# Two weight conversions moved between the stages of an attention and two-MoE kernel

## The chip, the cores and the metric

The kernel runs on one core of a Trainium2 chip. The metric is the device time of one execution in microseconds (us). Five engines of a core work side by side, each through its own instructions in their order: TensorE (PE), VectorE (DVE), ScalarE (ACT), GpSimd (POOL) and SyncE (SP), which issues all the DMA transfers here. They wait for one another by semaphores. An instruction whose input or whose buffer isn't ready holds up everything behind it on its engine.

## The reference

An attention over packed keys, then two layers called MoE, which are plain two-layer networks:

```python
p_packed = sm_attn(p, k, v)              # 8 batches, 8 heads, 576 positions, 64 wide
x = sm_attn(q, p_packed, p_packed)       # reshaped to 4608 x 512
h = x @ w_in1;  g = max(0.01*h, h);                y   = g @ w_out1   # 512 -> 2048 -> 512
h = y @ w_in2;  g = h / (1 + exp(-1.702*h));       out = g @ w_out2   # 512 -> 2048 -> 512
```

The weights come as 64-bit floats. The kernel turns them to 32 bits itself.

## The kernel before

**Stages.** (1) Attention and the first MoE's first layer, up to about 368 us; g goes to DRAM. (2) "y", the first MoE's second layer, 368 to 732 us. (3) "units", the second MoE's first layer, 732 to 1133 us. (4) "sum", its second layer, to the end.

**Seven products.** y, units and sum multiply 2 x 2 blocks by seven products instead of eight (`PRODUCTS`, in the order 1, 7, 5, 6, 2, 4, 3), with sums of the left and of the right quarters as operands. For each weight matrix, the seven combinations of its quarters are formed beforehand and put into a scratch in DRAM. Every operand is split into a high and a low part (fp32r): ScalarE casts the high part, DVE subtracts it from the value (L107). Each product is three matmuls: high x high, high x low, low x high.

**Steps.** The stages count in steps. In y a step is one slice of 128 of one product, 6 matmuls (line 650); a block of 768 tokens is 7 x 8 = 56 steps, and there are 6 blocks, so 336 steps. In the units a step is one product of one unit, also 6 matmuls (line 684); 48 units of 7 steps make 336 steps too. What is not matmul work stands in an agenda: `at(step, ...)` puts a piece at a step, and `side(step)` runs what is due there, in the order in which it was put there. So the order of each engine's instructions is a matter of these step numbers. `split(step, ...)` puts a cast on ScalarE at a step and the subtraction on DVE (L107) at the next.

**y.** For step k the left operand is cast at step k-3 and subtracted at k-2. DVE also forms the sums of quarters, each 768 wide: S3 at steps 1, 4, 7, 10 of a block (L480), S1 at 12, 14, 16, 19 (L482), S2 at 20, 22, 24, 27 (L484) and S4 at 34, 38, 42, 46 (L486), and adds results out of PSUM at the ends of products (L515 at step 23, L520 at 31, L525 at 47 and 55; L521 at 34 is without PSUM). In the last block, from step 28 on, `y_block` prepares the first block of y for the units as well, one piece every second step, and `new_weights` the first weights.

**Units.** Four pairs of PSUM banks. Products 1 and 2 of a unit share a bank, 7 and 4 another. ScalarE copies u out of the first after product 1 (L688) and v out of the second after product 7 (L690); the products 2 and 4, three steps later, go into the same banks behind these copies. `new_weights` converts the weights of the next unit pair in four pieces; `load_weights` fetches them from the scratch of w_in2. `y_block` prepares the next block of y in 14 pieces: slowly, every four steps (from steps 36 and 148), or fast, every one and a half (from steps 105 and 217). Each unit's g goes to DRAM two steps behind its end. From step 231 on, `weights` fetches and casts the first weights of sum ("early").

**A conversion.** `combined(what, first, late)` puts one `combine` of a 128-wide part at each step s of the list `first`: 16 for w_in2 (names wi), 16 for w_out2 (wo). Each has these pieces:
- s: three DMAs load the raw words (tile raw, one buffer; 512 KB in all).
- s+late: ScalarE's two casts L121 (into tile b) and L122 (into tile v).
- +1: DVE L125. +2: DVE L128, POOL's addition L129 into b.
- +5: DVE L144, L145. +6: DVE L147, L148.
- +7: the DMA that stores seven parts of b to the scratch (448 KB, L151).

Raw, v and b have one buffer each: the next conversion's loads wait for L128 of this one, and its L121 waits for this one's store to have landed.

Of the kernel before, what the change touches and what calls it, by code (L numbers as in the profile page):

```python
# [24 lines left out]
NJ = NF // 2  # L25
# [21 lines left out]
def packed_attention_moe_moe_kernel(tc, qT, kT, vm, vt, pT, w_in1, w_out1, w_in2, w_out2, out):  # L47
# [32 lines left out]
    with ExitStack() as ctx:  # L80
# [28 lines left out]
        def pieces(piece, steps):  # L109

            for step in steps:
                at(step, lambda: next(piece, None))
# [19 lines left out]
        def combine(name, source, scratch):  # L132


            conv = pools["conv"]
            raw = conv.tile([P, 4, 256], U32, tag="raw", name=f"raw_{name}")
            for i, (x, y) in enumerate(((0, 1), (0, 0))):
                nc.sync.dma_start(raw[:, i], source[:, x, y])
            nc.sync.dma_start(raw[:, 2:4], source[:, 1])
            yield  # L140
            b = conv.tile([P, 8, P], F32, tag="b", name=f"b_{name}")
            v = conv.tile([P, 4 * P], F32, tag="v", name=f"v_{name}")
            yield from to_f32(b[:, 0:4].rearrange("p i w -> p (i w)"), raw.rearrange("p i (w t) -> p (i w) t", t=2), v, True)
            nc.vector.tensor_sub(b[:, 4], b[:, 0], b[:, 1])  # L144
            nc.vector.tensor_sub(b[:, 5], b[:, 3], b[:, 0])  # L145
            yield
            nc.vector.tensor_sub(b[:, 6], b[:, 3], b[:, 4])  # L147
            nc.vector.tensor_sub(b[:, 7], b[:, 2], b[:, 6])  # L148
            if scratch is not wo1c:
                yield  # L150
                nc.sync.dma_start(place(name, scratch), b[:, 1:8])  # L151
                return
            yield
            h = pools["px"].tile([P, 2, 7, P], F32R, tag="hl", name=f"hl_{name}")
            nc.scalar.copy(h[:, 0], b[:, 1:8])
            yield
            nc.vector.tensor_sub(h[:, 1], b[:, 1:8], h[:, 0].bitcast(F32))
            yield
            for x in range(2):
                nc.sync.dma_start(place(name, scratch)[:, x], h[:, x].bitcast(F32))  # L160
# [2 lines left out]
            _, j, u = name.split("_")  # L163
            return scratch[int(j)][..., P * int(u):P * int(u) + P]

        def combined(what, first, late, start=0):

            view, to = {"wo1": (w_out1_v, wo1c), "wi2": (w_in2_v, wi2c), "wo2": (w_out2_v, wo2c)}[what]
            for n, s in enumerate(first, start):
                j, u = divmod(n, 2)  # L170
                src = view[:, :, u, :, j, :] if what == "wi2" else view[:, :, j, :, u, :]
                pieces(combine(f"{what}_{j}_{u}", src, to), (s, *(s + late + k for k in (0, 1, 2, 5, 6, 7, 8, 9))))
# [234 lines left out]
        for c in range(1, 4):  # L407
            for k in range(4):
                s = 8 * c - 8 + k
# [4 lines left out]
        for b in range(B):  # L414
            s = 32 * b
            if b + 1 < B:
                if b == 0:
                    first, second = (8, 9, 9, 10, 11, 12), range(14, 22)
                    third, fourth = range(22, 30), range(24, 32)
                else:  # L420
                    first, second = (-3, -2, -2, 0, 1, 2), range(5, 13)
# [7 lines left out]


        combined("wo1", range(30, 30 + 16 * 11, 11), 8)

        steps = [(blk, p, f) for blk in range(NBK) for p in PRODUCTS for f in range(NJ)]
# [40 lines left out]
        def prepare(nm, g):  # L474


            def combo(blk, fp, what):
                a11, a12, a21, a22 = (raws.get((blk, i, h, fp)) for i in range(2) for h in range(2))
                if what == "S3":
                    nc.vector.tensor_sub(a11, a11, a21)  # L480
                elif what == "S1":
                    nc.vector.tensor_add(a21, a21, a22)  # L482
                elif what == "S2":
                    nc.vector.tensor_sub(a11, a22, a11)  # L484
                else:
                    nc.vector.tensor_sub(a12, a12, a11)  # L486
                    load_raw(blk + 1, 0, 0, fp, nm, g)

            def high(k, blk, p, f):
                src = raws[(blk, *PLACE[p], f // 2)][:, f % 2, :]  # L490
                t = ga[blk, p, f] = pools["dr"].tile([P, 2, HB], F32R, tag=f"s{k % ROLL}", name=f"{nm}a_{blk}_{p}_{f}")
                nc.scalar.copy(t[:, 0, :], src)  # L492
                return t[:, 1, :], src, t[:, 0, :].bitcast(F32)

            for blk in range(NBK):
                s = 7 * NJ * blk
                for what, when in (("S3", (1, 4, 7, 10)), ("S1", (12, 14, 16, 19)), ("S2", (20, 22, 24, 27)), ("S4", (34, 38, 42, 46))):
                    for fp, k in enumerate(when):
                        at(s + k, lambda blk=blk, fp=fp, what=what: combo(blk, fp, what))
            for k, step in enumerate(steps):  # L500
                split(k - LEAD - 1, lambda k=k, step=step: high(k, *step))
                blk, p, f = step
                if f % 2 and p in (5, 4, 3):
                    at(k - LEAD, lambda blk=blk, p=p, f=f: load_raw(blk + 1, *PLACE[p], f // 2, nm, g))
# [34 lines left out]
        for k in range(EARLY):  # L539
            s = 32 * (B - 2) + 20 + 8 * k  # L540
# [29 lines left out]
        def y_block(early, steps, blk):  # L570

            t0 = TB * blk
            q = {}

            def load():
                for i, j in ((0, 0), (1, 0), (1, 1), (0, 1)):
                    home, tag = ("dr", f"r10{2 * i + j}") if blk == 0 else ("cy", f"y{2 * i + j}")
                    q[i, j] = pools[home].tile([P, 2, HB], F32, tag=tag, name=f"yq_{blk}_{i}{j}")
                    nc.sync.dma_start(q[i, j], yT[2 * j:2 * j + 2, :, t0 + HB * i:t0 + HB * i + HB].rearrange("d p t -> p d t"))

            def one(p, k):
                src, i = q[PLACE[p]], PRODUCTS.index(p)
                if blk not in ya:
                    ya[blk] = pools["ABC"[blk % 3]].tile([P, 7, 2, 2, HB], F32R, tag="ABC"[blk % 3], name=f"ya_{blk}")
                t = ya[blk][:, i]
                nc.scalar.copy(t[:, 0, k], src[:, k])
                return t[:, 1, k], src[:, k], t[:, 0, k].bitcast(F32)

            def combo(p):
                sub = nc.vector.tensor_sub  # L590
                if p == 1:
                    sub(q[0, 0], q[0, 0], q[1, 0])
                    nc.vector.tensor_add(q[1, 0], q[1, 0], q[1, 1])
                elif p == 7:
                    sub(q[0, 0], q[1, 1], q[0, 0])
                elif p == 6:
                    sub(q[0, 1], q[0, 1], q[0, 0])
            at(early, load)
            for n, step in enumerate(steps):
                p, k = (1, 2, 7, 5, 6, 4, 3)[n // 2], n % 2  # L600
                split(step, lambda p=p, k=k: one(p, k))
                if k:
                    at(step + 1, lambda p=p: combo(p))
# [29 lines left out]
        first_raws("b", g1)  # L633
        later_weights(lambda n: "w5" if n < 8 else "d", wo1c, "wo1")
        prepare("b", g1)
        combined("wi2", [56 * blk + k for blk in range(1, 5) for k in (-4, 14, 32)], 14)
        last = 7 * NJ * (NBK - 1)
        y_block(last + 24, range(last + 28, last + 56, 2), 0)
        side_until(0)
        for k, (blk, p, f) in enumerate(steps):  # L640
# [7 lines left out]
            for c in range(2):  # L648
                for m, (ws, xs) in enumerate(((0, 0), (0, 1), (1, 0))):
                    nc.tensor.matmul(acc[BANK[p]][:, c, :HB], lhsT=w[:, ws, P * c:P * c + P], rhs=x[:, xs, :],  # L650
                                     start=(p in OPENS and f + m == 0), stop=(f == NJ - 1 and m == 2), skip_group_check=True)
# [68 lines left out]
        for m in range(2, 3 * NJ - 1):  # L720
            late = (8 if (m + 1) % NJ == 2 else 4 if m == 2 else 0 if (m + 1) % NJ == 1 else 1)
            new_weights(range(14 * m + late, 14 * m + late + 4), m + 1)
        for q in range(2):
            s = 14 * NJ * q
            y_block(s + 28, range(s + 36, s + 92, 4), 2 * q + 2)
            y_block(s + 92, [s + 105 + 3 * n // 2 for n in range(14)], 2 * q + 3)
        combined("wi2", range(1, 49, 12), 11, 12)
        combined("wo2", range(49, 49 + 16 * 11, 11), 10)
        for k in range(EARLY):
            s = 7 * (4 * NJ + 2 * k + 1)  # L730
            weights(s, (s + 8, s + 12), k // 2, k % 2, None, wo2c, "wo2")
        at(7 * (6 * NJ - 3), *(lambda fp=fp: load_raw(0, 1, 0, fp, "d", g2) for fp in range(4)))
        at(7 * (6 * NJ - 1), *(lambda fp=fp: load_raw(0, 0, 0, fp, "d", g2) for fp in range(4)))
# [23 lines left out]
        for k, (blk, p, f) in enumerate(steps):  # L757
            side(k)
            x, w = ga.pop((blk, p, f)), wt[p, f // 4][:, :, f % 4]
            for c in range(3):  # L760
                b = acc4[BANK[p]][:, c // 2, 256 * (c % 2):256 * (c % 2) + 256]
                for m, (xs, ws) in enumerate(((0, 0), (0, 1), (1, 0))):
                    nc.tensor.matmul(b, lhsT=x[:, xs, P * c:P * c + P], rhs=w[:, ws, :],  # L763
                                     start=(p in OPENS and f == 0 and m == 0 and c != 1),
# [48 lines left out]
```

## Time and profile before

| what | value |
|---|---|
| median of 3 runs | 1504.54 us (1504.23 to 1504.83) |
| the profiled execution | 1506.49 us, its span 1504.7 us |
| PE busy | 1425.3 us, 95% of the span |
| DVE busy | 1102.7 us, 73% |
| ACT busy | 836.3 us, 56% |
| POOL busy | 95.8 us, 6% |
| L684, matmuls of the units | 2016, busy 369.9 us, idle before them 31.0 us |
| L650, matmuls of y | 1296 and 720, busy 231.0 and 128.9 us, idle before them 3.5 and 5.5 us |
| L763, matmuls of sum | 1944 and 1080, busy 233.2 and 132.4 us, idle before them 1.5 and 1.7 us |

Busy times say how long an engine had an instruction at work. Idle time before a group of instructions is the time for which their engine stood still ahead of them, and the releaser behind it is the instruction whose end let them start. Matmuls overlap, so a stretch is best judged by its length over its number of matmuls. PEld is the load of weights into the array, which precedes each matmul.

### The profile page before, as it was taken

Reading aid. Unit: us, or ns where it says so; the run is one execution under the profiler, and the core shown is the slowest. Engines: PE = TensorE matmul, PEld = TensorE weight load, DVE = VectorE, ACT = ScalarE, POOL = GpSimd, SP = SyncE. Lnnn points to the kernel's source line nnn. Section 1 sums busy time; section 2 is a strip of 40 time slices with the busy share of each in tenths; the row PEclk is TensorE's granted clock in tenths of the full one; section 3 lists DMA queues with packets and bytes.
Section 4 is the critical chain, followed back from the end, with each engine's and each line's share of the span. In section 5 each row is a group of like instructions: output and inputs, shape, how many; then the busy total and the mean of one; then the engine's idle time right before and its main releaser. Section 6 shows DMA issues by size and latency. Waiting matters only on the chain. (4 is left out here: it accounts for less than half of the span.)

```text
span 1504.7 us, 27724 instructions
## 1 busy us (share of the span) xinstructions
PE 1425.3 (95%) x10400; PEld 1329.5 (88%) x10400; DVE 1102.7 (73%) x2068; ACT 836.3 (56%) x1791; POOL 95.8 (6%) x71
## 2 busy tenths in 40 slices
PE   7789999999999999999999998889999999999998
PEld 4567777778999999999889988789999999999998
DVE  5667767762778888888877786676658987777876
ACT  3656666665555555455665665456655645445443
POOL 1310110000000101100011110100000000000000
PEclk7889999999999999999999999999999999999999
DMA  9459999969977366562466867585667524525321
GB/s 362 156 201 316 312 320 302 341 220 335 325 255 222 122 207 191 166 207 80 155 238 223 289 213 262 185 264 184 219 225 265 187 66 156 178 65 168 119 93 43
DMA packets 228773, 317.42 MB, mean 211 GB/s; under 512 B 12576, under 2 KB 188704, under 8 KB 228640
## 3 DMA queue, kind: packets, MB, share of 16 engines
q1 hardware_dynamic: 228640, 315.67, 63.0%
q8 instruction: 81, 1.33, 0.3%
q14 instruction: 52, 0.43, 0.1%
HBM read 191.89 MB, written 123.73 MB: 210 GB/s over the span
## 5 line engine op out<-in xcount | busy, mean ns | idle before, releaser
L684 PE MATMUL h<-ya,wj 128*128 128x384 f32 x2016 | 369.9, 344 | 31.0 <-ACT uv L688 13.7
L684 PEld LDWEIGHTS h<-ya,wj 128*128 128x128 f32 x2016 | 359.2, 192 | 41.5 <-ACT uv L688 17.7
L338 PEld LDWEIGHTS h<-a,m 128*128 128x128 f32 x1536 | 215.9, 195 | 53.5 <-ACT g L343 22.1
L338 PE MATMUL h<-a,m 128*128 128x288 f32 x1536 | 239.8, 309 | 9.3 <-ACT a L315 3.4
L492 ACT CAST da<-dr 128x384 fp32r<-128x384 f32 x336 | 166.4, 514 | 145.9 <-PE sum L763 108.1
L492 ACT CAST ba<-br 128x384 fp32r<-128x384 f32 x336 | 164.8, 514 | 142.7 <-PE y L650 83.4
L763 PE MATMUL sum<-wo,da 128*128 128x256 f32 x1944 | 233.2, 281 | 1.5 <-DVE da L107 1.3
L650 PE MATMUL y<-ba,wo 128*128 128x384 f32 x1296 | 231.0, 337 | 3.5 <-DVE ba L107 2.8
L763 PEld LDWEIGHTS sum<-wo,da 128*128 128x128 f32 x1944 | 231.0, 188 | 3.1 <-DVE da L107 3.1
L650 PEld LDWEIGHTS y<-ba,wo 128*128 128x128 f32 x1296 | 224.1, 188 | 9.5 <-DVE ba L107 8.4
L107 DVE TENSOR_TENSOR da<-dr,da 128x384 fp32r<-128x384 f32 x336 | 172.5, 552 | 40.9 <-ACT da L492 40.8
L107 DVE TENSOR_TENSOR ba<-br,ba 128x384 fp32r<-128x384 f32 x336 | 177.0, 565 | 32.3 <-ACT ba L492 32.2
L343 ACT ACTIVATE g<-h 128x288 f32<-128x288 f32 x256 | 105.4, 417 | 99.8 <-PE h L338 98.6
L650 PE MATMUL y<-ba,wo_early 128*128 128x384 f32 x720 | 128.9, 340 | 5.5 <-DVE ba L107 2.9
L763 PE MATMUL sum<-wo_early,da 128*128 128x256 f32 x1080 | 132.4, 285 | 1.7 <-ACT da L492 1.6
L763 PEld LDWEIGHTS sum<-wo_early,da 128*128 128x128 f32 x1080 | 131.5, 193 | 2.2 <-ACT da L492 1.9
L650 PEld LDWEIGHTS y<-ba,wo_early 128*128 128x128 f32 x720 | 126.3, 190 | 7.2 <-DVE ba L107 4.5
L327 DVE TENSOR_TENSOR m<-m,m 128x512 fp32r<-128x512 f32 x64 | 42.9, 683 | 54.8 <-ACT m L325 54.4
L129 POOL TENSOR_TENSOR b_wo<-v_wo,b_wo 128x512 int32<-128x512 int32 x32 | 43.1, 1348 | 418.6 <-DVE v_wo L128 248.7
L677 ACT ACTIVATE g<-cc 128x384 f32<-128x384 f32 x96 | 50.4, 525 | 29.1 <-DVE cc L700 26.2
L107 DVE TENSOR_TENSOR wj<-wjs,wj 128x512 fp32r<-128x512 f32 x88 | 54.5, 632 | 11.9 <-ACT wj L626 11.7
L129 POOL TENSOR_TENSOR b_wi<-v_wi,b_wi 128x512 int32<-128x512 int32 x16 | 30.4, 1898 | 447.6 <-DVE v_wi L128 347.6
(114 smaller groups left out, 1357.1 us busy)
## 6 DMA issues: line engine op xcount, KB each, us to landing
g_scratch<-g SPq DMA_DIRECT2D x64, 576.0 KB, 5.2
br<-g_scratch SPq DMA_DIRECT2D x96, 384.0 KB, 5.5
g_scratch<-g SPq DMA_DIRECT2D x96, 384.0 KB, 4.6
dr<-g_scratch SPq DMA_DIRECT2D x96, 384.0 KB, 4.4
wjs<-wi_scratch SPq DMA_DIRECT2D x22, 896.0 KB, 5.3
wo_scratch<-hl_wo SPq DMA_DIRECT2D x32, 448.0 KB, 5.9
wo<-wo_scratch SPq DMA_DIRECT2D x27, 512.0 KB, 8.7
k<-in_kT_dram SPq DMA_DIRECT2D x16, 576.0 KB, 6.6
```

Of the source, the lines that this page charges most:

```text
L107: at(step + 1, lambda: nc.vector.tensor_sub(*rest))
L129: nc.gpsimd.tensor_tensor(d, v.bitcast(I32), d, op=ALU.add)
L327: nc.vector.tensor_sub(m[:, 1, par, :], t[par], m[:, 0, par, :].bitcast(F32))
L338: nc.tensor.matmul(t[:, :TH], lhsT=m[:, ws, par, o:o + P], rhs=a[:, xs, par, :], start=(k == 0), stop=(k == 5))
L343: nc.scalar.activation(g1t[g][:, f % 2, hf * TH:hf * TH + TH], t[:, :TH], AF.Prelu, alpha=0.01)
L492: nc.scalar.copy(t[:, 0, :], src)
L650: nc.tensor.matmul(acc[BANK[p]][:, c, :HB], lhsT=w[:, ws, P * c:P * c + P], rhs=x[:, xs, :], start=(p in OPENS and f + m == 0), stop=(f == ...
L677: nc.scalar.activation(g[f][:, HB * i:HB * i + HB], src, AF.Gelu_apprx_sigmoid)
L684: nc.tensor.matmul(b, lhsT=w[:, ws, c, P * kk:P * kk + P], rhs=x[:, xs, kk, :], start=(p in OPENS and kk + s == 0), stop=(kk + s == 3), sk ...
L763: nc.tensor.matmul(b, lhsT=x[:, xs, P * c:P * c + P], rhs=w[:, ws, :], start=(p in OPENS and f == 0 and m == 0 and c != 1), stop=(f == NJ ...
```

## The change

Three lists of steps change, and a parameter that is no longer needed goes.

```diff
-        def combined(what, first, late, start=0):
+        def combined(what, first, late):
...
-        combined("wi2", [56 * blk + k for blk in range(1, 5) for k in (-4, 14, 32)], 14)
+        combined("wi2", [26, 44] + [56 * blk + k for blk in range(1, 5) for k in (1, 19, 38)] + [281, 299], 14)
...
-        combined("wi2", range(1, 49, 12), 11, 12)
-        combined("wo2", range(49, 49 + 16 * 11, 11), 10)
+        combined("wo2", range(3, 3 + 16 * 15, 15), 10)
         for k in range(EARLY):
-            s = 7 * (4 * NJ + 2 * k + 1)
+            s = 7 * (4 * NJ + 2 * k + 2)
```

- w_in2's 16 conversions all stand in y now: two that load in block 0 (steps 26 and 44), three in each of blocks 1 to 4 (at their steps 1, 19, 38 instead of -4, 14, 32), two in the last block (its steps 1 and 19). Before, the last four stood in the units, at steps 1, 13, 25, 37.
- w_out2's 16 conversions start at step 3 of the units instead of 49 and come every 15 steps instead of 11. The last loads at 228 instead of 214.
- The early weights of sum are fetched and cast one unit (7 steps) later.

The number of instructions of each kind stays the same.

ScalarE in the units, around units 20 and 21, before. b_wo and v_wo are the targets of a conversion's casts L121 and L122, uv those of the copies L688 and L690, g the results, ya the prepared y.

```order
L677 ACTIVATE g_20_1_9923<-uv_9920 128x384
L677 ACTIVATE g_20_0_9922<-cc_9921 128x384
L688 COPY uv_10003<-h_8312 128x384
L121 ACTIVATE b_wo_4_0_10014<-raw_wo_4_0_9895 128x512
L122 ACTIVATE v_wo_4_0_10015<-raw_wo_4_0_9895 128x512
L677 ACTIVATE g_20_1_9923<-cc_9921 128x384
L690 COPY uv_10003<-h_8313 128x384
L586 CAST ya_10026<-yq_00_9931 128x384
```

The same place now:

```order
L677 ACTIVATE g_20_1_9943<-uv_9940 128x384
L677 ACTIVATE g_20_0_9942<-cc_9941 128x384
L688 COPY uv_10019<-h_8376 128x384
L677 ACTIVATE g_20_1_9943<-cc_9941 128x384
L690 COPY uv_10019<-h_8377 128x384
L586 CAST ya_10038<-yq_00_9951 128x384
L121 ACTIVATE b_wo_4_1_10040<-raw_wo_4_1_9926 128x512
L122 ACTIVATE v_wo_4_1_10041<-raw_wo_4_1_9926 128x512
```

The conversion that stood between the two copies of one unit stands behind both now. With 15 steps between conversions and units of 7 steps, their place in a unit moves on by one step each time, so that others stand between the copies.

SP's queue in the units, where raw_wo is a load of raw words, b_wo the store of a finished conversion, wjs the next weights and g_scratch the stores of g, before:

```order
L614 DMA wjs_10151<-wi_scratch 128x1792
L138 DMA raw_wo_5_0_10154<-in_w_out_dram 128x256 x2
L139 DMA raw_wo_5_0_10154<-in_w_out_dram 128x2x256
L710 DMA g_scratch<-g_22_0_10086 128x768
L710 DMA g_scratch<-g_22_1_10087 128x768
L151 DMA wo_scratch<-b_wo_4_1_10138 896x1x128
L138 DMA raw_wo_5_1_10274<-in_w_out_dram 128x256 x2
L139 DMA raw_wo_5_1_10274<-in_w_out_dram 128x2x256
```

And now:

```order
L138 DMA raw_wo_5_0_10093<-in_w_out_dram 128x256 x2
L139 DMA raw_wo_5_0_10093<-in_w_out_dram 128x2x256
L151 DMA wo_scratch<-b_wo_4_1_10040 896x1x128
L710 DMA g_scratch<-g_21_0_10021 128x768
L710 DMA g_scratch<-g_21_1_10022 128x768
L614 DMA wjs_10163<-wi_scratch 128x1792
L710 DMA g_scratch<-g_22_0_10100 128x768
L710 DMA g_scratch<-g_22_1_10101 128x768
L138 DMA raw_wo_5_1_10257<-in_w_out_dram 128x256 x2
L139 DMA raw_wo_5_1_10257<-in_w_out_dram 128x2x256
```

The next loads of raw words stand farther behind the store.

DVE in the last block of y, steps 15 to 21 (br are the quarters with their sums, ba the subtracted left operands), before:

```order
L482 TENSOR_TENSOR br_102_7299<-br_102_7299,br_112_7559 128x768
L107 TENSOR_TENSOR ba_5_2_7852<-br_101_7277,ba_5_2_7852 128x384
L107 TENSOR_TENSOR ba_5_3_7864<-br_101_7277,ba_5_3_7864 128x384
L107 TENSOR_TENSOR ba_5_4_7873<-br_102_7299,ba_5_4_7873 128x384
L482 TENSOR_TENSOR br_103_7320<-br_103_7320,br_113_7579 128x768
L107 TENSOR_TENSOR ba_5_5_7882<-br_102_7299,ba_5_5_7882 128x384
L484 TENSOR_TENSOR br_000_7457<-br_110_7513,br_000_7457 128x768
```

And now:

```order
L107 TENSOR_TENSOR ba_5_2_7888<-br_101_7299,ba_5_2_7888 128x384
L125 TENSOR_SCALAR raw_wi_7_0_7750<-raw_wi_7_0_7750 128x512
L107 TENSOR_TENSOR ba_5_3_7904<-br_101_7299,ba_5_3_7904 128x384
L128 SCALAR_TENSOR_TENSOR v_wi_7_0_7891<-v_wi_7_0_7891,raw_wi_7_0_7750 128x512
L107 TENSOR_TENSOR ba_5_4_7914<-br_102_7299,ba_5_4_7914 128x384
L482 TENSOR_TENSOR br_103_7349<-br_103_7349,br_113_7611 128x768
L107 TENSOR_TENSOR ba_5_5_7925<-br_102_7299,ba_5_5_7925 128x384
L484 TENSOR_TENSOR br_000_7480<-br_110_7542,br_000_7480 128x768
L107 TENSOR_TENSOR ba_5_6_7935<-br_103_7349,ba_5_6_7935 128x384
L144 TENSOR_TENSOR b_wi_7_0_7890<-b_wi_7_0_7890 128x128
L145 TENSOR_TENSOR b_wi_7_0_7890<-b_wi_7_0_7890 128x128
```

A conversion's DVE instructions stand where there was none. In blocks 1 to 4 a conversion stood some five steps earlier and now stands at this place.

## Rows read from the trace of the kernel before

**Rows 1.** Stretches: us, busy of PE, PEld, DVE, ACT, POOL; clock; DMA share; GB/s.
```profile
367.80:428.60 60.80, 60.49 (x336) 59.92 (x337) 45.71 (x78) 30.99 (x62) 0.00 (x0) 0.97 1.02 344
...
732.20:758.40 26.20, 23.33 (x122) 20.63 (x121) 21.29 (x38) 17.30 (x37) 1.47 (x1) 1.00 0.62 214
758.40:1056.80 298.40, 270.24 (x1457) 262.44 (x1457) 213.28 (x439) 172.41 (x378) 25.69 (x19) 0.96 0.69 233
1056.80:1133.10 76.30, 76.29 (x438) 75.98 (x438) 41.41 (x77) 41.22 (x87) 0.00 (x0) 1.00 0.67 224
```
**Rows 2.** Groups by line, 758.4 to 1056.8: busy, mean ns | idle before, releasers.
```profile
L684 PE MATMUL h<-ya,wj 128*128 128x384 f32 x1457 | 270.2, 346 | 28.6 <-ACT uv L688 13.4 <-ACT uv L690 11.7 <-DVE uv L692 2.3
```
**Rows 3.** Timeline of PE in the units: start, us, what [idle before, releaser].
```profile
861.32 7.73 PE L684 MATMUL h<-ya,wj 128*128 128x384 f32 x42 [1.38 <-ACT uv L688]
...
881.96 28.00 PE L684 MATMUL h<-ya,wj 128*128 128x384 f32 x156 [0.81 <-DVE uv L692]
```
**Rows 4.** Waits of ACT, 735 to 1136: us in total, times, longest.
```profile
ACT b_wo L121 <- DMA wo_scratch<-b_wo: 28.7, 10, 5.9
```
**Rows 5.** Timeline of all engines around 910 us.
```profile
907.82 0.56 SPq L151 DMA_DIRECT2D wo_scratch<-b_wo  x1
...
914.25 0.66 ACT L121 ACTIVATE b_wo<-raw_wo 128x512 int32<-128x512 uint32 x1 [2.84 <-DMA wo_scratch<-b_wo]
...
915.76 0.47 ACT L690 COPY uv<-h 128x384 f32<-128x384 f32 x1
...
916.28 5.92 PE L684 MATMUL h<-ya,wj 128*128 128x384 f32 x19 [3.50 <-ACT uv L690]
```
**Rows 6.** The tile b_wo, 735 to 1136: its stores.
```profile
DMA to landing us min/median/max: 3.3/5.0/9.1
```
**Rows 7.** One stretch of 8 us; columns as in rows 1.
```profile
916.00:924.00 8.00, 7.72 (x31) 7.72 (x32) 7.60 (x14) 4.18 (x10) 1.28 (x1) 0.66 0.47 164
```
**Rows 8.** Groups by line of DVE, 758.4 to 1056.8; columns as in rows 2.
```profile
L128 DVE SCALAR_TENSOR_TENSOR v_wo<-v_wo,raw_wo 128x512 uint32<-128x512 uint32 x16 | 11.0, 686 | 0.1
L125 DVE TENSOR_SCALAR raw_wo<-raw_wo 128x512 uint32<-128x512 uint32 x16 | 6.9, 428 | 39.3 <-ACT v_wo L122 39.3
...
L144 DVE TENSOR_TENSOR b_wo<-b_wo 128x128 f32<-128x128 f32 x16 | 4.5, 284 | 3.2 <-POOL b_wo L129 3.2
```
**Rows 9.** Timeline of DVE in block 2 of y, which starts at 488.7.
```profile
489.05 0.95 DVE L525 TENSOR_TENSOR c<-u,y 128x768 f32<-128x768 f32 x1 [1.08 <-PE y L650]
...
491.26 1.49 DVE L107 TENSOR_TENSOR ba<-br,ba 128x384 fp32r<-128x384 f32 x3
...
506.73 0.29 DVE L144 TENSOR_TENSOR b_wi<-b_wi 128x128 f32<-128x128 f32 x1 [1.19 <-POOL b_wi L129]
```
**Rows 10.** Timeline of POOL: the first and the second conversion of block 2.
```profile
503.39 3.30 POOL L129 TENSOR_TENSOR b_wi<-v_wi,b_wi 128x512 int32<-128x512 int32 x1 [19.11 <-DVE v_wi L128]
523.08 1.48 POOL L129 TENSOR_TENSOR b_wi<-v_wi,b_wi 128x512 int32<-128x512 int32 x1 [16.39 <-DVE v_wi L128]
```
**Rows 11.** Timeline of PEld: block 2 of y (from 488.68), last block (from 669.51).
```profile
488.68 18.91 PEld L650 LDWEIGHTS y<-ba,wo_early 128*128 128x128 f32 x109
508.61 1.88 PEld L650 LDWEIGHTS y<-ba,wo_early 128*128 128x128 f32 x11 [1.02 <-DVE ba L107]
...
517.44 11.41 PEld L650 LDWEIGHTS y<-ba,wo 128*128 128x128 f32 x66 [0.41 <-DVE ba L107]
...
669.51 20.82 PEld L650 LDWEIGHTS y<-ba,wo_early 128*128 128x128 f32 x120
...
697.19 8.30 PEld L650 LDWEIGHTS y<-ba,wo 128*128 128x128 f32 x48 [0.45 <-DVE ba L107]
```
**Rows 12.** Timeline of DVE in the last block of y.
```profile
687.77 1.03 DVE L107 TENSOR_TENSOR ba<-br,ba 128x384 fp32r<-128x384 f32 x2 [1.00 <-ACT ba L492]
...
694.85 0.95 DVE L515 TENSOR_TENSOR v<-v,y 128x768 f32<-128x768 f32 x1 [1.10 <-PE y L650]
...
699.60 1.03 DVE L107 TENSOR_TENSOR ba<-br,ba 128x384 fp32r<-128x384 f32 x2 [0.19 <-ACT ba L492]
```

More of the change, by code (lines that the diff above doesn't have):

```diff
@@ L164, in place @@
             return scratch[int(j)][..., P * int(u):P * int(u) + P]
-        def combined(what, first, late, start=0):
+        def combined(what, first, late):
             view, to = {"wo1": (w_out1_v, wo1c), "wi2": (w_in2_v, wi2c), "wo2": (w_out2_v, wo2c)}[what]
-            for n, s in enumerate(first, start):
+            for n, s in enumerate(first):
                 j, u = divmod(n, 2)
```

## The prediction

> **What bounds the kernel now.** I read the table of stages first. The second MoE's first layer (the units, line 684) runs from 732.2 to 1133.1 us, 400.9 us in all [rows 1]. Its last 438 matmuls take 76.30 us, 0.1742 us each, and nothing holds them up; at that pace the 1457 matmuls from 758.4 to 1056.8 would take 253.8 us, and they took 298.4: 44.6 us lost. The 122 matmuls of the start took 26.2 instead of 21.3 us, 5 us lost. So about 50 us of this stage are not matmul work, and the conversions of w_out2 and of the rest of w_in2 lie in the middle stretch. A step (6 matmuls) is 1.045 us.
>
> What is lost there: the groups by line put 28.6 us of idle time before these 1457 matmuls, 25.1 of it ended by ScalarE's copies L688 and L690 out of PSUM [rows 2]. A bank's next product may not start before its copy, and there are only three steps (3.1 us) between them, so ScalarE may be no more than that late. ScalarE's waits say why it is late: ten times, 28.7 us in all, L121 waited for the store of the conversion before, because b has a single buffer [rows 4]. One case in full [rows 5]: the store is issued at 907.82; L121 comes up at 911.4 and may start only at 914.25, 2.84 us later; the copy L690 stands behind it in ScalarE's order and starts at 915.76; PE, idle for 3.50 us, goes on at 916.28. The arithmetic fits: a conversion that loads at s casts at s+10 and stores at s+17, and the next casts at s+21. Four steps are 4.2 us, and a store takes 3.3 to 9.1 us to land, 5.0 in the median [rows 6].
>
> The clock comes on top. After that 3.50 us gap the granted clock is 0.66 over 8 us [rows 7]: some two thirds of them at 1.2 GHz instead of 2.4. The mean of 0.96 over 298.4 us [rows 1] is about 12 us at most, less what falls on gaps where PE stood anyway; I take 10. So 44.6 is roughly 30 us of waiting (the 28.6, and a little that the row hides: a matmul is shown for 0.346 us at a pitch of 0.174, so each gap is shown some 0.17 short), 10 of clock and 5 of small delays.
>
> **The change, part by part.**
> *Spacing 15.* The next cast comes at s+25, eight steps (8.4 us) behind the store. That covers all landings but the longest (9.1 us), so the 28.7 us of waits go, and the gaps over 2.6 us with their low clock. The raw load moves off its predecessor too: at s+11 it had to wait in SP's queue for L128 at s+12, with stores of g and loads of wjs behind it; at s+15 its tile has been free for three steps. Instructions per conversion stay the same.
> What stays in the middle stretch: (a) The first fast preparation of y (steps 105 to 126, 861 to 882 us), where DVE and ScalarE are overfull: five gaps, the first of 1.38 us and the last of 0.81, 3.65 in all [rows 3]. Two conversions fall into it before and after. I keep 3 us, and 2.5 for its repetition at step 217. Ends: 0, if the slack of three steps takes it, and 3.65 each with a low clock behind it, some 11 for both. (b) 2 us of small delays. In all 7.5 us of 44.6 stay: 37 us gained. The 5 us of the start are kept, since conversion casts there move by one step only.
> *Four conversions into y's first and last block, and the others moved inside their blocks.* Price on DVE: 0.43 for L125, 0.69 for L128, four subtractions of 0.28 [rows 8], 2.24 us; in a full row three L107 take 1.49 us and two 1.03 [rows 9, 12], so each adds 0.46 and begins some 0.1 before the last one's end; six of them make that 1.8. To that comes POOL's addition: the first conversion of a block, amid DVE work on SBUF alone, had it run 3.30 us and DVE stood still for 1.19 us at L144; the second, with DVE's PSUM addition beside it, 1.48 us and no such wait [rows 9, 10]. So 1.8 to 3.0 us for each conversion where DVE is full.
> The Trainium skill, "SBUF — State Buffer", section on the shared ports' single rule, says that a DVE instruction with two SBUF inputs and a GpSimd instruction that reads SBUF exclude each other for the whole instruction. By it, the conversions between steps 16 and 21 and between 34 and 39 pay the full 3.0 us, as no PSUM addition stands between their L128 and L144; by the second row alone it would be 1.8, and the sum 3 to 8 us lower.
> The value I take is 3.0, as in the row of the full stretch.
> Blocks 1 to 4: the first conversion moves from DVE steps 11 to 16 to steps 16 to 21. What it cost: PE's weight load of step 26 stands at 517.44, 28.76 us after the block's start, and in the last block, with none, 27.68 after it [rows 11]: 1.08 us. What it will cost: 3.0, less the 0.34 of L125 that fits into DVE's wait of 1.00 for ScalarE there, less the 1.10 that DVE waits for PE at step 23 in the free block [rows 12]: 1.56. So +0.5 per block, 2.0 for four. The second conversion moves from steps 29 to 34 to 34 to 39; as full a stretch as before, so I take 0, between a gain of 0.5 and a loss of 1.5 per block. The third lies around the block's border, where DVE waits 1.08 us for PE's last product [rows 9].
> Block 0: two loads more. DVE is busy 45.7 of 60.8 us there [rows 1], and that idle time hides the first (without it 3.0). The second's DVE part falls into block 1's steps 3 to 8 and leaves DVE late where the next conversion comes: 1.5 us, between 0 and 3.0.
> Last block: nothing hides them. DVE is the bound from step 29 on (it prepares y for the units as well; its only break is 0.19 us, [rows 12]). The first costs 1.56, less that 0.19; the second its full 3.0: 4.4 us; lowest 1.8.
> In all y grows by 2.0 + 1.5 + 4.4 = 7.9, say 8 us; between 2 (0 for blocks 0 to 4, 1.8 for the last) and 20 (four times 2.0, twice 3.0, twice 3.0).
> *DMAs and queues.* The raw load at step 57 waits in SP's queue for L128 at step 60; behind it stand stores and loads due at 62 and later, so nothing. The last store of w_out2 is issued at step 245, its reader's load at 252, seven steps later. POOL has nothing else. The early weights move by one unit, into a stretch without other conversions.
> Sum against the profiled execution's 1506.49 us (span 1504.7): 37 less, 8 more, so 1477.5. The median of the runs shown is 1504.54, 1.95 lower: 1475.5.
>
> **The rivals.**
> (B) *The engines, not the store.* Once the store's wait is gone, DVE takes its place: it is busy 213 of 298 us in the stretch [rows 1]; over 261 us that is 82% before the four conversions leave, and it works in bursts. For it: the five gaps of rows 3, which no wait for a store explains. Against it: in the last 438 matmuls, with the early weights to convert beside the units, PE loses nothing. It would leave half of the gain, 18: 1504.5 - 18 + 8 = 1494.
> (C) *Slower.* The waits for the store only stand where ScalarE, held by DVE, would wait anyway; then the stage gains just the work that leaves, 4 x 3.0 = 12 us. If y pays from its full price (20 us), the time is 1504.5 - 12 + 20 = 1512; it decides from the point where y's price exceeds the units' gain. Against it: the case of [rows 5], where only the store stood between ScalarE and its copy.
> A rule of the Trainium skill speaks for (C): "DMA: Bandwidth & Descriptors", the fixed and variable cost of a transfer, gives about 2 us plus the bytes over 436 GB/s, fitted on transfers that GpSimd issues. For the 448 KB of a store that would be an estimate of 3.1 us, under the four steps, and the old spacing would have had no wait to remove. The trace disagrees: 5.0 us in the median, 9.1 at most [rows 6].
> (D) *More.* The slack takes both fast preparations, the clock stays high throughout and y pays 4: 1504.5 - 44 + 4 = 1464.5.
>
> **How the numbers follow.** Forecast 1475.5 with a chance of 0.55, (D) 0.2, (B) 0.18, (C) 0.07. The forecast's own range is 1468 to 1484 (5 us on the gain, 4 on y). For 8 in 10 it reaches to (D) and to (B): 1462 to 1494, leaving out (C), half of (B)'s upper side and the far end of (D). A measurement of this kernel tells some 0.2%, 3 us, from no change. Faster by more: 0.92, all but (C) and a remnant; slower 0.06; within 0.02.
>
> **What would show it.** Right: in the units no wait of L121 for wo_scratch over 1 us; idle before L684 in the middle under 10 us instead of 28.6; the granted clock at 1.00 through the middle; the stage 362 to 366 us long. In y, the step-18 wait (1.02 at 508.61, [rows 11]) gone from blocks 2 to 4, the one at step 26 near 2 us in all, the last block 66 to 67 us instead of 62.5 from weight load to weight load. Wrong: waits of L690 with no store before them (B); gaps above 2.6 us with a low clock behind them; a last block over 70 us or blocks 1 to 4 over 63 (C).

## The result, and the profile after

The changed kernel takes 1487.66 us (median of 4 runs, 1484.06 to 1489.18), the kernel before beside it 1504.38 (4 runs). The ratio is 0.9892, with an interval of 0.9866 to 0.9918: about 17 us faster. The forecast was 1475.5 us, with 1462 to 1494 as the range. So the direction is right and the range holds the time, but 12 us of the expected 29 are missing.

The profiled execution took 1488.2 us (span 1486.4). I cut both traces at the first weight load of y, of the units and of sum, and y at the first weight load of each block:

| us | before | after | difference | forecast |
|---|---|---|---|---|
| until y | 367.83 | 367.05 | -0.8 | 0 |
| y, block 0 | 60.60 | 72.27 | +11.7 | 0 |
| y, block 1 | 60.25 | 61.77 | +1.5 | +0.5 and +1.5 |
| y, blocks 2 to 4 together | 180.83 | 182.78 | +2.0 | +1.5 |
| y, last block | 62.52 | 67.12 | +4.6 | +4.4 |
| units | 402.68 | 366.19 | -36.5 | -37 |
| sum, to the end of the span | 369.99 | 369.22 | -0.8 | 0 |

Every term but one is within 1 us of the forecast. Block 0 alone holds the error.

The stretches of the changed kernel, with the columns of [rows 1]: block 0 of y, then start, middle and end of the units.

```profile
367.05:439.32 72.27, 63.03 (x336) 61.73 (x336) 48.80 (x84) 31.75 (x64) 1.43 (x1) 0.91 1.00 335
750.99:776.00 25.01, 22.19 (x121) 20.52 (x121) 20.23 (x35) 16.88 (x36) 1.26 (x1) 1.00 0.68 246
776.00:1039.00 263.00, 259.08 (x1458) 255.85 (x1459) 209.01 (x416) 167.63 (x367) 19.97 (x15) 0.99 0.73 247
1039.00:1115.60 76.60, 76.58 (x441) 76.16 (x440) 42.01 (x79) 42.06 (x90) 0.00 (x0) 1.00 0.68 224
```

The middle has one matmul more than in [rows 1], takes 263.0 us instead of 298.4, and its clock is 0.99 instead of 0.96. The end has the old pace (76.60 / 441 = 0.1737 us). The start loses 25.01 - 121 x 0.1742 = 3.9 us, where it lost 5 before.

The same middle by line, as in [rows 2]: busy, mean ns | idle before, releasers.

```profile
L684 PE MATMUL h<-ya,wj 128*128 128x384 f32 x1458 | 259.4, 339 | 5.5 <-DVE uv L692 2.4 <-DVE ya L107 2.4 <-DVE wj L107 0.4
```

ScalarE's waits in the units, as in [rows 4] (us in total, times, longest), and the landing of the stores, as in [rows 6]:

```profile
ACT b_wo L121 <- DMA wo_scratch<-b_wo: 2.0, 3, 1.0
```

```profile
DMA to landing us min/median/max: 3.3/4.6/7.9
```

The 28.6 us of idle time have become 5.5, and none of its three largest parts is ended by a copy of ScalarE's. L121 waited for a store 28.7 us in ten cases, now 2.0 in three. The stores land hardly sooner (5.0 and 4.6 us in the median): they are waited for less because the next cast comes four steps later.

**Where the missing 12 us are.** PE in block 0 of the changed kernel (start, us, what, [idle before, releaser]):

```profile
407.71 7.79 PE L650 MATMUL y<-ba,wo 128*128 128x384 f32 x44
423.75 0.69 PE L650 MATMUL y<-ba,wo 128*128 128x384 f32 x1 [8.25 <-ACT ba L492]
425.15 14.51 PE L650 MATMUL y<-ba,wo 128*128 128x384 f32 x71 [0.71 <-DVE ba L107]
```

ScalarE at that place:

```profile
412.07 0.52 ACT L492 CAST ba<-br 128x384 fp32r<-128x384 f32 x1
422.09 0.66 ACT L121 ACTIVATE b_wi<-raw_wi 128x512 int32<-128x512 uint32 x1 [9.50 <-DMA raw_wi<-in_w_in_dram]
422.65 0.65 ACT L122 ACTIVATE v_wi<-raw_wi 128x512 f32<-128x512 f32 x1
423.20 2.15 ACT L492 CAST ba<-br 128x384 fp32r<-128x384 f32 x5
```

SP's queue ahead of it, and then the longest wait of SP between 365 and 415 us:

```profile
370.76 1.40 SPq L347 DMA_DIRECT2D g_scratch<-g  x2
...
381.11 11.02 SPq L450 DMA_DIRECT2D wo<-wo_scratch  x10
...
407.08 5.51 SPq L450 DMA_DIRECT2D wo<-wo_scratch  x4
412.63 2.54 SPq L138 DMA_DIRECT2D raw_wi<-in_w_in_dram  x2
415.22 0.55 SPq L139 DMA_DIRECT2D raw_wi<-in_w_in_dram  x1
```

```profile
SPq L450 <- DMA g_scratch<-g: 8.9, 1, 8.9
```

Read backwards: the raw words of block 0's first conversion belong to step 26, which begins near 394.7 us (156 matmuls of 0.1742 after 367.6). SP issued their load at 412.63, 18 us later. It had stood for 8.9 us, from 372.2 to 381.1, waiting for a store of g to land, and then issued one load after another. L121 comes up at step 40 and waited 9.50 us for the words. Five casts of y's own left operand, L492, stand behind it in ScalarE's order and ran only when it was done. PE used up what had been cast before and stood still for 8.25 us.

Three stretches of the same block, with the columns of [rows 1]:

```profile
405.00:415.00 10.00, 10.00 (x60) 10.00 (x59) 6.37 (x11) 4.10 (x8) 0.00 (x0) 1.00 1.09 356
415.00:425.00 10.00, 1.19 (x4) 0.47 (x3) 1.67 (x3) 2.91 (x7) 0.00 (x0) 0.71 1.08 372
425.00:435.00 10.00, 9.85 (x46) 9.85 (x47) 9.19 (x18) 3.94 (x8) 1.43 (x1) 0.78 0.92 284
```

The clock is 0.71 in the stretch with the gap and 0.78 in the one behind it, so part of the time at 1.2 GHz. The 71 matmuls from 425.15 took 14.51 us, 0.204 each instead of 0.174: 2.1 us more. With the gaps of 8.25 and 0.71 that makes 11.1 of the 11.7 us.

**The last block of y**: weight loads at its start, at step 26 and at the start of the units, to be held against [rows 11].

```profile
683.87 20.82 PEld L650 LDWEIGHTS y<-ba,wo_early 128*128 128x128 f32 x120
...
712.99 8.31 PEld L650 LDWEIGHTS y<-ba,wo 128*128 128x128 f32 x48 [0.64 <-DVE ba L107]
...
750.99 1.06 PEld L684 LDWEIGHTS h<-ya,wj 128*128 128x128 f32 x6
```

Step 26 begins 29.12 us after the block's start; without a conversion it was 27.68. So the first costs 1.44 us (1.56 less 0.19 were forecast) and the second the rest of the 4.6, some 3.2 (3.0 were forecast). How GpSimd and VectorE share these two conversions, POOL first:

```profile
703.42 1.48 POOL L129 TENSOR_TENSOR b_wi<-v_wi,b_wi 128x512 int32<-128x512 int32 x1 [19.53 <-DVE v_wi L128]
726.33 4.22 POOL L129 TENSOR_TENSOR b_wi<-v_wi,b_wi 128x512 int32<-128x512 int32 x1 [21.43 <-DVE v_wi L128]
```

```profile
703.67 2.05 DVE L482 TENSOR_TENSOR br<-br,br 128x768 f32<-128x768 f32 x1
...
706.11 0.95 DVE L484 TENSOR_TENSOR br<-br,br 128x768 f32<-128x768 f32 x1
...
730.58 0.29 DVE L144 TENSOR_TENSOR b_wi<-b_wi 128x128 f32<-128x128 f32 x1 [1.18 <-POOL b_wi L129]
```

In the first, POOL ran at its short time and DVE's sum L482, begun 0.25 us later, took 2.05 us instead of the 0.95 that a sum of the same shape takes at 706.11. In the second, POOL took 4.22 us and DVE waited 1.18 for it at L144. So DVE lost 1.1 to 1.2 us either way. This agrees with the rule of the Trainium skill, "SBUF — State Buffer", on the shared ports, that such a pair excludes each other: one of the two pays. The trace also bears out the 3.0 us taken for a conversion without a PSUM addition beside it: 1.8 for its own instructions and the 1.10 by which L482 was longer make 2.9. Of the 3.0 the prediction took off the breaks of DVE at that place, 0.34, 1.10 and 0.19, and the 1.37 left are near the 1.44 measured. Which of the two is held up, the start times do not tell. In block 2 of the kernel before, an L107, POOL's addition ([rows 10]) and the sum L482 began at the same distances from one another (503.18, 503.39 and 503.64) as in the last block here (703.21, 703.42 and 703.67), and there POOL took 3.30 us and the sum 0.95. DVE in that block 2:

```profile
503.18 0.55 DVE L107 TENSOR_TENSOR ba<-br,ba 128x384 fp32r<-128x384 f32 x1
503.64 0.95 DVE L482 TENSOR_TENSOR br<-br,br 128x768 f32<-128x768 f32 x1
```

### The profile page after: what moved, and what is told of

The parts are those of the page before. It is cut to its first block, busy times and chain, and to the rows that moved or that the text cites. A ratio compares the mean times of both kernels' runs of the same rounds, so it can differ in the third digit from the quotient of the medians.

```text
span 1486.4 us, 27714 instructions
## 1 busy us (share of the span) xinstructions
PE 1417.2 (95%) x10400; PEld 1322.9 (89%) x10400; DVE 1107.5 (75%) x2068; ACT 836.2 (56%) x1791; POOL 100.4 (7%) x71
## 4 chain that ended last, share of the span: by engine, by line
PE 71%; DVE 17%; issue 4%; DMA 3%; ACT 2%; POOL 2%; SPq 1%; DVEq 0%; ACTq 0%; POOLq 0%
PE sum L762 23%; PE h L684 20%; PE y L650 14%; PE h L338 10%; DVE ba L107 3%; PE m L218 2%; POOL b_wi L129 1%; PE pp L273 1%; PE s L218 1%; DVE m L327 1%; DVE br L482 1%; DVE br L484 1%; DVE wj L107 1%; DVE ya L107 1%; DVE da L107 1%
## 5 line engine op out<-in xcount | busy, mean ns | idle before, releaser
L684 PE MATMUL h<-ya,wj 128*128 128x384 f32 x2016 | 357.7, 338 | 6.7 <-DVE uv L692 2.4
L684 PEld LDWEIGHTS h<-ya,wj 128*128 128x128 f32 x2016 | 352.5, 189 | 11.7 <-DVE uv L692 4.1
L650 PE MATMUL y<-ba,wo 128*128 128x384 f32 x1296 | 238.1, 341 | 19.6 <-DVE ba L107 10.9
L492 ACT CAST ba<-br 128x384 fp32r<-128x384 f32 x336 | 164.5, 513 | 149.7 <-PE y L650 89.8
L492 ACT CAST da<-dr 128x384 fp32r<-128x384 f32 x336 | 166.3, 514 | 145.2 <-PE sum L762 105.4
L107 DVE TENSOR_TENSOR da<-dr,da 128x384 fp32r<-128x384 f32 x336 | 172.8, 554 | 40.5 <-ACT da L492 40.4
L107 DVE TENSOR_TENSOR ba<-br,ba 128x384 fp32r<-128x384 f32 x336 | 175.7, 556 | 25.5 <-ACT ba L492 25.5
L129 POOL TENSOR_TENSOR b_wo<-v_wo,b_wo 128x512 int32<-128x512 int32 x32 | 42.5, 1330 | 485.5 <-DVE v_wo L128 367.6
L107 DVE TENSOR_TENSOR wj<-wjs,wj 128x512 fp32r<-128x512 f32 x88 | 55.8, 647 | 9.7 <-ACT wj L626 9.7
L692 DVE TENSOR_TENSOR uv<-uv,h 128x384 f32<-128x384 f32 x48 | 26.5, 553 | 46.5 <-PE h L684 39.9
## 6 DMA issues: line engine op xcount, KB each, us to landing
br<-g_scratch SPq DMA_DIRECT2D x96, 384.0 KB, 7.0
g_scratch<-g SPq DMA_DIRECT2D x96, 384.0 KB, 5.4
dr<-g_scratch SPq DMA_DIRECT2D x96, 384.0 KB, 4.3
```

The source lines that it names most:

```text
L107: at(step + 1, lambda: nc.vector.tensor_sub(*rest))
L129: nc.gpsimd.tensor_tensor(d, v.bitcast(I32), d, op=ALU.add)
L684: nc.tensor.matmul(b, lhsT=w[:, ws, c, P * kk:P * kk + P], rhs=x[:, xs, kk, :], start=(p in OPENS and kk + s == 0), stop=(kk + s == 3), sk ...
L692: nc.vector.tensor_add(v, v, b)
```

## The experiments

Theory 1 is that the units gain because L121 no longer waits for the store, that y pays VectorE's time, and that block 0's loss is the late load and the in-order wait behind it. The ratios are to the kernel before on the same chip.

| kernel | us (lowest to highest) | ratio and interval | y | block 0 | last block | units |
|---|---|---|---|---|---|---|
| e1 | 1476.71 (1475.05 to 1481.95) | 0.9812 (0.9787 to 0.9837) | 376.2 | 62.7 | 67.8 | 365.9 |
| e2 | 1468.58 (1467.64 to 1471.18) | 0.9755 (0.9735 to 0.9775) | 364.6 | 60.9 | 62.5 | 368.5 |
| e3 | 1518.34 (1515.46 to 1523.77) | 1.0095 (1.0065 to 1.0124) | 384.0 | 71.9 | 67.7 | 395.7 |
| e4 | 1475.15 (1474.07 to 1476.01) | 0.9808 (0.9791 to 0.9825) | 373.8 | 62.1 | 67.3 | 363.7 |
| e5 | 1469.80 (1468.01 to 1470.60) | 0.9772 (0.9754 to 0.9789) | 368.7 | 61.6 | 62.5 | 363.8 |
| e6 | 1465.83 (1465.50 to 1466.17) | 0.9748 (0.9728 to 0.9767) | 364.2 | 60.5 | 62.5 | 365.9 |

The last four columns are lengths in each profiled execution, cut as above. The medians of before were 1505.45 us beside e1 to e3 and 1504.24 beside e4 to e6.

**e1, the load of block 0's first conversion early.** Only its three DMAs move, from step 26 of y to step 230 of the attention stage; the casts stay at step 40.

```diff
-                pieces(combine(f"{what}_{j}_{u}", src, to), (s, *(s + late + k for k in (0, 1, 2, 5, 6, 7, 8, 9))))
+                piece = combine(f"{what}_{j}_{u}", src, to)
+                if what == "wi2" and n == 0:
+                    piece = first_wi2
+                else:
+                    at(s, lambda piece=piece: next(piece, None))
+                pieces(piece, [s + late + k for k in (0, 1, 2, 5, 6, 7, 8, 9)])
...
+        first_wi2 = combine("wi2_0_0", w_in2_v[:, :, 0, :, 0, :], wi2c)
+        at(230, lambda: next(first_wi2))
```

> The changed kernel, with one move: the first conversion of w_in2 loads its raw words at step 230 of the attention stage instead of step 26 of y's block 0; its casts stay at step 40. Theory 1 (block 0's loss is ScalarE standing at L121 for a load that left late in a full DMA queue): the 8.25 us gap of PE in block 0 is gone, with the low clock behind it, and block 0 takes 60 to 62 us instead of 71.7; the whole about 1477. Rival (the conversion's own work on DVE, ScalarE and POOL costs it): block 0 stays over 68 us, the whole at 1485 to 1488.

Measured: 1476.71 us. The load, the cast and PE in block 0, of SP, of ScalarE and of PE:

```profile
339.71 0.98 SPq L138 DMA_DIRECT2D raw_wi<-in_w_in_dram  x2
```

```profile
410.49 0.68 ACT L121 ACTIVATE b_wi<-raw_wi 128x512 int32<-128x512 uint32 x1
```

```profile
387.96 28.00 PE L657 MATMUL y<-ba,wo 128*128 128x384 f32 x157
416.21 10.88 PE L657 MATMUL y<-ba,wo 128*128 128x384 f32 x59 [0.26 <-DVE ba L107]
```

L121 no longer waits, and PE has no gap over 0.3 us inside the block. The block takes 62.7 us instead of 72.3, a little more than the 60 to 62 expected: 9.6 us were the late load. 2.1 us remain over the 60.6 of before (1.5 in e4 and 1.0 in e5, with the same load), 1.2 of them in four short waits of the weight loads for DVE. The remainder follows the clock at y's start, before the conversion's casts: over the first 28 us of y it was 0.89 in e1, 0.94 in e4 and in the kernel before, and 1.00 in e5. So even without the late load block 0 was not free. Block 1 and the last block were 1.2 and 0.7 us longer in this execution than in the changed kernel's, which leaves 7.7 us in y; in e4 it is 10.1.

**e2, a second buffer for b in the kernel before.** The second operand v moves into b's upper half to make room; the steps stay as before.

```diff
-            b = conv.tile([P, 8, P], F32, tag="b", name=f"b_{name}")
-            v = conv.tile([P, 4 * P], F32, tag="v", name=f"v_{name}")
+            b = conv.tile([P, 8, P], F32, tag="b", name=f"b_{name}", bufs=2)
+            v = b[:, 4:8].rearrange("p i w -> p (i w)")
```

> The kernel before, with two buffers for a conversion's result b instead of one (v lies in the part of b that is still unused then); spacing 11 and all places stay. Theory 1 (the units lost their time to L121 waiting for the store before it): those 28.7 us of waits go, the units take 366 to 375 us instead of 400.9, the clock in their middle is at 0.99 or 1.00, y stays as before; the whole about 1472. Rival B (engines too full at spacing 11): the waits of L121 go, but PE's gaps behind L688, L690 or L692 stay at over 15 us; the whole 1490 or more.

Measured: 1468.58 us, 36.9 less than before. The landing of the stores of w_out2's conversions, and PE in the units by line:

```profile
DMA to landing us min/median/max: 3.3/4.9/8.8
```

```profile
L684 PE MATMUL h<-ya,wj 128*128 128x384 f32 x2014 | 358.6, 339 | 7.7 <-ACT uv L688 1.8 <-ACT uv L690 1.6 <-DVE ya L107 1.5
```

The stores take as long as before, the conversions come every 11 steps as before, and four more of them stand in the units than in the changed kernel. Still the idle time falls from 31.0 to 7.7 us and the stage from 402.7 to 368.5, since nothing waits for a store: L121 has no row among ScalarE's waits any more. This shows the cause of the units' loss, and rival (B), the engines, falls.

**e3, y's part of the change alone.** w_in2's conversions as in the changed kernel, w_out2's as before.

```diff
-        combined("wi2", [56 * blk + k for blk in range(1, 5) for k in (-4, 14, 32)], 14)
+        combined("wi2", [26, 44] + [56 * blk + k for blk in range(1, 5) for k in (1, 19, 38)] + [281, 299], 14)
...
-        combined("wi2", range(1, 49, 12), 11, 12)
```

> The kernel before with one part of the change: all 16 conversions of w_in2 in y as in the changed kernel, those of w_out2 as before (from step 49, every 11 steps). Theory 1: y pays what it pays in the changed kernel (block 0 71.7 us, blocks 1 to 4 61 to 62, last block 67; together 19.6 us more), the units lose only the part of four conversions (some 3 to 6 us less than 400.9), so the whole is 1517 to 1522. Rival C (the units gain by the four conversions that leave, not by the spacing): the units fall to 375 us or less, the whole is 1500 or less.

Measured: 1518.34 us. Its waits of ScalarE in the units, PE there by line, and PE in block 0:

```profile
ACT b_wo L121 <- DMA wo_scratch<-b_wo: 28.0, 10, 5.5
```

```profile
L684 PE MATMUL h<-ya,wj 128*128 128x384 f32 x1997 | 362.3, 341 | 28.3 <-ACT uv L688 15.1 <-ACT uv L690 9.3 <-DVE uv L692 1.1
```

```profile
421.82 0.69 PE L650 MATMUL y<-ba,wo 128*128 128x384 f32 x1 [8.00 <-ACT ba L492]
```

y pays its 20 us, with the same gap in block 0, while the units keep their waits of 28 us and gain only 7.0 us by the four conversions that left (3 to 6 were expected). Alone this part of the change makes the kernel slower. Rival (C) took the gain to be no more than that of the conversions that leave: the other 29.5 us come with w_out2's new steps. The early weights, which move by one unit together with them, were not tried by themselves.

**e4, the changed kernel with e1's load and e2's second buffer together.** Its edits are those of e1 and e2.

> The changed kernel with the early load of e1 and, in addition, two buffers for the conversion's result b (its second operand v lies in b's upper half, as in e2). Theory 1 (the spacing of 15 and the second buffer remove one and the same wait, that of L121 for the store): nothing is left to remove, the units stay 364 to 366 us long and the time that of e1, 1474 to 1479 us. Rival E (the two edits add up, because the single buffer also costs something that the row of L121 does not show): the units fall to 358 us or less, 1465 to 1470.

Measured: 1475.15 us. The units, with the columns of [rows 1]:

```profile
739.75:1103.41 363.66, 357.57 (x2018) 352.91 (x2017) 271.00 (x530) 227.42 (x495) 21.32 (x16) 1.00 0.72 243
```

The time is e1's within both ranges; the units are 2.3 us shorter than e1's and 2.5 shorter than the changed kernel's, about the 3.0 and 2.0 us for which L121 still waited there. Spacing and buffer remove one and the same wait.

**e5, e4 with the two conversions of the last block back in the units**, and those of w_out2 behind them, every 13 steps.

```diff
-        combined("wi2", [26, 44] + [56 * blk + k for blk in range(1, 5) for k in (1, 19, 38)] + [281, 299], 14)
+        combined("wi2", [26, 44] + [56 * blk + k for blk in range(1, 5) for k in (1, 19, 38)], 14)
...
-        combined("wo2", range(3, 3 + 16 * 15, 15), 10)
+        combined("wi2", (1, 16), 11, 14)
+        combined("wo2", range(31, 31 + 16 * 13, 13), 10)
```

> e4 with the last two conversions of w_in2 taken out of the last block of y and put into the units again (loads at steps 1 and 16, casts 11 steps later), w_out2 behind them from step 31 on, every 13 steps. Theory 1 (the last block pays for these two because VectorE is full there; the units have room for them): the last block goes from 67 back to 62 to 63 us, the units grow by 0 to 2 us, 1470 to 1474. Rival F (the last block's length comes from the shift of the conversions before it or from the preparation of the units, not from its own two): it stays above 65.5 us, and the time at 1475 to 1479.

Measured: 1469.80 us. First weight loads of the last block and of the units, in e4 and then in e5:

```profile
672.47 20.82 PEld L657 LDWEIGHTS y<-ba,wo_early 128*128 128x128 f32 x120
...
739.75 1.41 PEld L691 LDWEIGHTS h<-ya,wj 128*128 128x128 f32 x8
```

```profile
671.54 20.82 PEld L657 LDWEIGHTS y<-ba,wo_early 128*128 128x128 f32 x120
...
734.08 2.10 PEld L691 LDWEIGHTS h<-ya,wj 128*128 128x128 f32 x12
```

The last block falls from 67.28 to 62.54 us, and the units take 363.8 instead of 363.7. So the last block's growth came from its own two conversions. A conversion that costs 2.4 us there costs nothing that shows in the units.

**e6, e2 with w_out2 every 12 steps, and the early weights a unit later.**

```diff
-        combined("wo2", range(49, 49 + 16 * 11, 11), 10)
+        combined("wo2", range(49, 49 + 16 * 12, 12), 10)
...
-            s = 7 * (4 * NJ + 2 * k + 1)
+            s = 7 * (4 * NJ + 2 * k + 2)
```

> e2 (the kernel before with two buffers for b) with w_out2's conversions every 12 steps instead of 11 and the early weights one unit later. Theory 1 (with the store's wait gone the spacing is worth nothing more): the units stay 365 to 367 us, 1466 to 1470 as e2. Rival G (the places of the casts in ScalarE's order have a price of their own, the waits for L688 and L690 that e2 still shows, 5.2 us before weight loads): up to 4 us less, 1462 to 1465.

Measured: 1465.83 us, between the two expectations. The units, with the columns of [rows 1], and what is left of the weight loads' waits for L690 (2.5 us in e2):

```profile
729.56:1095.45 365.89, 357.87 (x2018) 352.59 (x2017) 277.22 (x554) 232.34 (x503) 26.69 (x20) 1.00 0.75 253
```

```profile
PEld h L684 <- ACT uv L690: 1.0, 2, 0.6
```

The stage is 2.6 us shorter than in e2, but the ratios of the two kernels overlap, and each ran beside another set of runs of before. Whether the spacing is worth 2 us of its own stays open. e6 has the lowest time here and beats both kernels: it takes the whole gain of the units and pays nothing in y.

## Why the prediction was right and wrong

- **Units, -37: right, and for its reason.** The stage took 366.2 us to the first weight load of sum, and 364.6 to the end of its matmuls (750.99 to 1115.60), within the forecast 362 to 366. e2 removes the wait without the spacing and gains 34.2 us; e4 shows that the two together gain little more than either. In the middle 7.5 us were to stay, and 263.0 - 1458 x 0.1742 = 9.0 stayed.
- **Signs in the units: right, but for the clock.** No wait of L121 over 1.0 us, idle time under 10 us. The clock came to 0.99 in the middle, not to 1.00. One sign of being wrong came as well, though in y and not in the units: a gap over 2.6 us with a low clock behind it, the 8.25 us in block 0.
- **Blocks 1 to 4: right.** +0.5 each was forecast; blocks 2 to 4 grew by 0.60 to 0.68, and block 1 by 1.5 where 0.5 and the 1.5 carried over from block 0 were forecast. The signs came too: the wait of 1.02 us at step 18 is gone from blocks 2 to 4, where the first 120 weight loads take 20.82 us without a break, and the four waits around step 26 add up to 2.0 us in block 2.
- **Last block, +4.4: right.** It grew by 4.6, split 1.4 and 3.2; e5 gives 4.7 back by taking the two conversions out.
- **Block 0, "that idle time hides the first (without it 3.0)": the step that failed.** It grew by 11.7 us. The step weighed only VectorE's instructions, at 0 to 3.0 us. It left out that the conversion begins with a load in SP's queue, and that the cast which waits for it stands ahead of y's casts in ScalarE's order. The paragraph on DMAs and queues looked at the load of block 1 (step 57) and not at those of steps 26 and 44. e1 gives the parts: 9.6 us for the late load and the wait behind it, and 2.1 that remain (1.0 to 2.1 over e1, e4 and e5), within the 3.0 of the step's bracket. With this term y grew by 19.7 us, the top of the 2 to 20 that were given for it, but by a cause that none of those bounds stood for. The time, 1487.66, lies outside the forecast's own 1468 to 1484 and inside 1462 to 1494 only because that range was drawn out to (B). To that extent it was luck that the range held.
- **Rivals.** The time lies nearer to (B), 1494, than to the forecast, but (B)'s mechanism is not there: with the store's wait gone, PE's idle time in the middle is 5.5 us, where (B) left half of the loss. (C) is refuted by e3; (D) fell short on both sides, 36.5 us in the units instead of 44, and 19.7 in y instead of 4.

It could have been seen in the trace of the kernel before. SP's queue there, at the same place:

```profile
371.52 1.41 SPq L347 DMA_DIRECT2D g_scratch<-g  x2
...
381.64 1.46 SPq L450 DMA_DIRECT2D wo<-wo_scratch  x3
...
406.97 5.51 SPq L450 DMA_DIRECT2D wo<-wo_scratch  x4
412.59 1.65 SPq L471 DMA_DIRECT2D br<-g_scratch  x1
```

SP stood from 372.9 to 381.6 and issued the last of the same loads of w_out1 until 412.5. The load of step 26 is put right behind them, so its time of issue could be read there without the change: 412.6. L121 is due at step 40, which begins at 367.8 + 40 x 1.045 = 409.6. Had the load taken as long as the stores of [rows 6], 3.3 to 9.1 us, L121 would have waited from 6.3 to 12.1 us; 9.5 came.

## What to carry to other kernels

When a step is moved, look up where its first instruction's queue really is at the new place: the order of SP's list is given by step numbers, but in this trace SP was 18 us behind them. Then ask what is queued behind the instruction that waits for this transfer; a load that costs no time itself took 9.6 us here because y's casts stood behind the cast that needed it. And where a wait comes from a single buffer, a second one (here 4 KB more in each partition, less the 2 KB of v that moved into it) took the wait away at every spacing tried (11, 12, 13 and 15 steps), without work that has to be moved elsewhere.

## What was not expected of the hardware

The first stage differs by some us between executions of the same instructions. The first 361 us of the kernel before and of e3, which changes nothing there, with the columns of [rows 1]:

```profile
3.00:364.00 361.00, 332.34 (x3336) 257.18 (x3337) 231.54 (x480) 218.09 (x518) 42.74 (x32) 0.94 0.84 285
```

```profile
3.00:364.00 361.00, 330.72 (x3344) 256.59 (x3344) 231.66 (x480) 218.95 (x520) 42.72 (x32) 0.96 0.85 287
```

VectorE's work is the same to 0.2 us; the clock is 0.94 and 0.96, and y begins at 367.83 and 365.44. In e1 it begins at 364.05, so that 3.0 of the 11.1 us between the spans of the changed kernel (1486.4) and of e1 (1475.3) lie ahead of y. Lengths of stages tell more here than whole spans do.

In blocks 1 to 4 and the last block of the changed kernel, a VectorE addition beside a GpSimd addition of 1.48 us took 2.05 us instead of 0.95, without a wait in any row: such a price shows only as a longer instruction.
